# Reordering batch 0's prologue in a fused linear-attention and SwiGLU kernel, with two loads exchanged and one eviction postponed

One core of a Trainium2 chip. The metric is device time in microseconds (us), the median of several executions; lower is better. A "fast run" is one not in a slow state.

## The reference

Linear attention with the feature map phi(x) = elu(x) + 1, then a gated feed-forward block. Batch 8, 8 heads, 576 positions, head size 64; 4608 tokens, model width 512, hidden width 1536; float32 in and out (the kernel multiplies in fp16).

```python
k_p, q_p = phi(k), phi(q)                    # phi(x) = where(x > 0, x, exp(x) - 1) + 1
kv  = einsum('bhsd,bhse->bhde', k_p, v)
z   = sum(k_p, axis=2)
x   = (q_p @ kv) / (q_p @ z + 1e-6)          # heads side by side: 4608 x 512
out = (silu(x @ w_gate) * (x @ w_val)) @ w_out
```

phi(k) is computed as max(k, 0) + min(exp(k), 1): `kp` holds the max, `ek` the min, and `add_k` puts their sum into `kp`. A matmul that sums over positions can therefore take the sum, or the two terms one after the other into the same accumulator.

## The kernel before

Everything runs in a hand-written order: each engine executes its instructions in the order of the program. Batch 0 is done first, as fast as possible, to give the first layer ("layer 1", `l1`) its input; from then on TensorE is busy without a break. Heads are handled in two halves (`lp` 0 and 1). PSUM is the memory that TensorE writes its results to; copying a result out of it frees the tile, and is called an eviction. The helpers that matter:

```python
def warm(n, w=512, ps=None): ...             # matmuls on ones: keep TensorE's clock up, result unused
def add_k(b, lp): ...                        # VectorE: kp += ek
def mn_k(b, lp): ...                         # VectorE: ek = min(ek, 1)
def zt(b, lp, ps, t, first, last): ...       # TensorE: column sums of t (9 matmuls of 2 columns)
def zr_copy(b, lp, ps): ...                  # VectorE: scaled copy of the sums, Zr
def kv_corner(b, lp, t, first, last): ...    # TensorE: k.v of a half, 36 matmuls of 64x64
def r_copy(b, l0, l1, engs): ...             # k.v out of PSUM, R
def t_corners(g, W, lp, ps): ...             # TensorE: q times Zr (denominator) or R (numerator)
def lnrd(ps, i): ...                         # ScalarE: 1/denominator as exp(-log)
def x_t(g, lp, ps): ...                      # VectorE: numerator times that: x, two chunks
def l1_mm(g, fb, ps, chunks): ...            # TensorE: layer 1, gate and value, on some of x's 4 chunks
```

The loads' order and the stretch of batch 0 that the change touches:

```python
    ...
    ld_w1(1280, 1536)
    ld(k, kr, 1, 1)
    ld_w2(0, 4)
    ld(q, qr, 1, 0)
    ld_w2(4, 8)
    ld(q, qr, 1, 1)
    ld_w2(8, 12)
    ld2(v, vr, 1)
    ...
    zt(0, 0, X[1], kp, True, False)
    warm(WARM[3])
    zt(0, 0, X[1], ek, False, True)
    zr_copy(0, 0, X[1])
    warm(WARM[4])
    t_corners(0, Zr, 0, pp4[2])
    lnrd(pp4[2], 0)
    q_phi(1, 1, qb)
    mn_k(0, 1)
    zt(0, 1, Y[0], kp, True, False)
    warm(WARM[5])
    zt(0, 1, Y[0], ek, False, True)
    add_k(0, 0)
    zr_copy(0, 1, Y[0])
    warm(WARM[6])
    kv_corner(0, 0, kp, True, True)
    t_corners(0, Zr, 1, Y)
    lnrd(Y, 1)
    r_copy(0, 0, 1, "VV")
    add_k(0, 1)
    t_corners(0, R, 0, X)
    x_t(0, 0, X)
    kv_corner(0, 1, kp, True, True)
    r_copy(0, 1, 2, "VV")
    warm(WARM[7], ps=pp4[2][1])
    l1_mm(0, 0, pp4[2], (0,))
    l1_mm(0, 1, X, (0,))
    t_corners(0, R, 1, pp4[1])
    x_t(0, 1, pp4[1])
    for c in (1, 2, 3):
        l1_mm(0, 0, pp4[2], (c,))
    ...
```

The end of layer 2 of period 0, where the input of period 1 is made (`nx`) between output tiles:

```python
        for t in range(4):
            ...
            if t == 3:
                nx(0, dz)                    # corners and the x products of period 1
                nx(1, cq)
            for fb in range(FO, FB):
                l2_mm(0, t, fb)
            if t < 3:
                l2_out(0, t, "V")            # VectorE: output tile out of PSUM
        exp_k(2, 0)
        exp_k(2, 1)
        l2_out(0, 3, "V")
```

## Time and profile before

| | before |
|---|---|
| median of three runs | 314.52 us (314.24 to 314.89) |
| span of the traced run | 312.5 us |
| first scale copy `Zr` (VectorE) | 10.11 us |
| first layer-1 matmul | 14.34 us |
| layer 1 in steady state (17th layer-1 matmul) | 18.28 us |
| layer 2 starts, first transposes | 35.54, 40.77 us |
| first and third layer-1 matmul of period 1 | 49.84, 50.44 us |

All times in the traces count from the start of the span. The first loads land at slightly different times in each execution, and shift all that follows (the first scale copy starts at 9.96 to 10.55 us in the traces below). So I compare stretches between two events of one trace: from the first scale copy to steady layer 1 (8.16 us before), the idle time ahead of the first transposes (their start, less the start of the matmul before them, less 0.216), and from the transposes to the third matmul of period 1 (9.67). The profile's lines are in the prediction.

### The profile page before, as it was taken

What the parts mean: (1) busy time and instruction counts of PE and PEld (TensorE: products, weight loads), DVE (VectorE), ACT (ScalarE), POOL (GpSimd) and SP (SyncE); (2) the same over time, 40 slices, a digit from 0 to 9 for tenths busy, and PEclk for the clock granted to TensorE, in tenths of its full rate; (3) what the DMA queues carried; (4) which work ended last, traced back from release to release, by engine and by line L of the source; (5) the groups of instructions that cost most, each with busy time, mean ns of one, the idle gap of its engine ahead of it and who ended that gap; (6) DMA issues with size and microseconds to landing.
All of it is one profiled execution on the core that took longest, in us unless ns stands there. A gap on an engine that the chain in (4) does not pass through costs nothing.

```text
span 312.5 us, 5494 instructions
## 1 busy us (share of the span) xinstructions
PE 306.2 (98%) x2169; PEld 142.3 (46%) x2169; DVE 204.0 (65%) x361; ACT 153.9 (49%) x232; POOL 47.4 (15%) x72
## 2 busy tenths in 40 slices
PE   8999999999999999999999999999999999999994
PEld 3444454444544454445444544454444444444442
DVE  4854859899699657976697759874981434143410
ACT  4955869639733845375535643475330333133311
POOL 8655334310000410032000500000000000000000
PEclk9999999999999999999999999999999999999999
DMA  8999999997512594139612990324032300140014
GB/s 218 198 196 200 207 206 240 231 206 127 116 26 41 92 192 117 38 50 183 171 37 39 131 235 3 73 45 92 2 69 57 86 1 1 39 97 0 0 36 101
DMA packets 41162, 32.80 MB, mean 105 GB/s; under 512 B 16432, under 2 KB 36144, under 8 KB 41136
## 3 DMA queue, kind: packets, MB, share of 16 engines
q0 software_dynamic: 20464, 18.29, 37.4%
q1 hardware_dynamic: 20592, 14.13, 18.8%
q8 instruction: 17, 0.28, 0.4%
q14 instruction: 9, 0.07, 0.1%
q10 hardware_dynamic: 80, 0.03, 0.0%
HBM read 37.75 MB, written 9.44 MB: 151 GB/s over the span
## 4 chain that ended last, share of the span: by engine, by line
PE 95%; DMA 1%; DVE 1%; ACT 1%; issue 0%; SPq 0%; DVEq 0%
PE pp L292 57%; PE pp L299 30%; PE pp L276 2%; PE pp L254 2%; PE pp L185 2%; DMA q<-in_q_dram 1%; PE pp L124 0%; ACT ek L120 0%; PE pp L398 0%; PE pp L370 0%; PE pp L429 0%; DVE xT L411 0%; ACT qT L120 0%; DVE kp L159 0%; PE pp L212 0%
## 5 line engine op out<-in xcount | busy, mean ns | idle before, releaser
L120 ACT ACTIVATE sil<-pp 128x512 f16<-128x512 f32 x108 | 63.4, 597 | 101.8 <-PE pp L292 100.0
L292 PE MATMUL pp<-xT,wg 128*128 128x512 f16 x416 | 106.8, 379 | 0.0
L292 PE MATMUL pp<-xT,wv 128*128 128x512 f16 x416 | 106.8, 379 | 0.0
L285 DVE SCALAR_TENSOR_TENSOR hT<-pp,sil 128x512 f16<-128x512 f32 x108 | 72.4, 681 | 48.8 <-PE pp L292 35.5
L299 PE MATMUL pp<-wo,hT 128*128 128x512 f16 (+2 forms) x444 | 97.1, 373 | 0.6 <-DVE osb L322 0.6
L299 PEld LDWEIGHTS <-hT 128*128 128x128 f16 x444 | 42.0, 98 | 49.8 <-issue 2.1
L292 PEld LDWEIGHTS <-wv 128*128 128x128 f16 x416 | 40.7, 98 | 49.1
L292 PEld LDWEIGHTS <-wg 128*128 128x128 f16 x416 | 40.7, 98 | 48.4
L322 DVE TENSOR_SCALAR osb<-pp 128x512 f32<-128x512 f32 (+1 forms) x19 | 12.9, 682 | 30.9 <-PE pp L299 26.5
L120 ACT ACTIVATE osb<-pp 128x512 f32<-128x512 f32 (+1 forms) x18 | 10.3, 574 | 34.8 <-PE pp L299 34.8
L120 ACT ACTIVATE ek<-kr 128x1152 f16<-128x1152 f16 x16 | 17.9, 1157 | 0.1
L120 ACT ACT_TABLE_LOAD x13 | 16.7, 1283 | 2.3 <-PE pp L292 2.1
L229 DVE TENSOR_TENSOR qp<-qp,rden 128x1152 f16<-128x1152 f16 x12 | 16.2, 1347 | 0.0
L220 DVE TENSOR_REDUCE den<-prod 128x18 f32<-128x1152 f16 x12 | 16.1, 1343 | 0.0
L120 ACT ACTIVATE eq<-qr 128x1152 f16<-128x1152 f16 (+1 forms) x15 | 16.0, 1102 | 0.1
L695 POOL COPY gate<-qT 128x1 f16<-128x1 f16 x4 | 1.0, 256 | 97.2 <-DMA qT<-qp 97.2
L271 DVE TENSOR_SCALAR xT<-pp 128x512 f16<-128x512 f32 (+1 forms) x14 | 8.8, 667 | 7.1 <-PE pp L254 7.1
L103 POOL DMA_DIRECT2D vr<-in_v_dram x16 | 11.7, 731 | 8.5 <-PE pp L292 2.6
L103 POOL DMA_DIRECT2D kr<-in_k_dram x16 | 11.5, 723 | 8.9 <-DMA vr<-in_v_dram 2.8
L159 DVE TENSOR_TENSOR kp<-ek,kp 128x1152 f16<-128x1152 f16 x16 | 12.1, 758 | 0.5
L103 POOL DMA_DIRECT2D qr<-in_q_dram x14 | 10.3, 736 | 6.7 <-DMA wo<-in_moe_w_out_dram 1.7
L147 DVE TENSOR_SCALAR ek<-ek 128x1152 f16<-128x1152 f16 x16 | 7.5, 470 | 5.7 <-ACT ek L120 5.5
(82 smaller groups left out, 179.5 us busy)
## 6 DMA issues: line engine op xcount, KB each, us to landing
out_dram<-osb SPq DMA_DIRECT2D x70, 128.0 KB, 3.4
kr<-in_k_dram POOLq DMA_DIRECT2D x16, 288.0 KB, 8.6
vr<-in_v_dram POOLq DMA_DIRECT2D x16, 288.0 KB, 9.9
qr<-in_q_dram POOLq DMA_DIRECT2D x14, 288.0 KB, 11.9
wo<-in_moe_w_out_dram POOLq DMA_DIRECT2D x3, 512.0 KB, 13.0
wg<-in_moe_w_gate_dram POOLq DMA_DIRECT2D x5, 256.0 KB, 8.7
wv<-in_moe_w_val_dram POOLq DMA_DIRECT2D x5, 256.0 KB, 9.3
q<-in_q_dram SPq DMA_DIRECT2D x2, 576.0 KB, 4.1
```

The costliest lines, as they stand in the source:

```text
L103: nc.gpsimd.dma_start(out=dst[b % NB][:, 2 * lp:2 * lp + 2, :], in_=src[b].rearrange("(l a) (c j) d -> (a c) l (j d)", a=2, j=J)[:, 2 * lp ...
L120: nc.scalar.activation(out=out, in_=in_, func=func, bias=bias, scale=scale)
L147: nc.vector.tensor_scalar(out=a, in0=a, scalar1=1.0, scalar2=None, op0=ALU.min)
L159: nc.vector.tensor_tensor(out=a, in0=ek[b % 2][:, lp, :, :], in1=a, op=ALU.add)
L185: nc.tensor.matmul(out=ps[hh][D * l2:D * l2 + D, D * lp:D * lp + D], lhsT=t[b % 2][rows, lp, j, D * l2:D * l2 + D], rhs=vr[b % NB][rows, 2 ...
L220: nc.vector.tensor_reduce(out=den[:, c, :], in_=prod[:, :, :].rearrange("p j (l d) -> p (j l) d", d=D), axis=AX.X, op=ALU.add)
L229: nc.vector.tensor_tensor(out=qv, in0=qv, in1=rden[:, c, :].unsqueeze(2).to_broadcast([P, 2 * J, D]), op=ALU.mult)
L271: nc.vector.tensor_scalar(out=dst, in0=ps[l2][:, c0:], scalar1=1.0 / SC, scalar2=None, op0=ALU.mult)
L285: nc.vector.scalar_tensor_tensor(out=hT[g % 2][:, fb, :], in0=ps[1][:, :], scalar=SC, in1=s[:, :], op0=ALU.mult, op1=ALU.mult)
L292: nc.tensor.matmul(out=ps[h][:, :], lhsT=w[:, c, P * fb:P * fb + P], rhs=xT[g % 2][:, c, :], start=(c == 0), stop=(c == 3))
L299: nc.tensor.matmul(out=l2p[(g, t)][:, n0:n1], lhsT=hT[g % 2][:, fb, P * t:P * t + P], rhs=wo[:, fb, n0:n1], start=(fb == 0), stop=(fb == F ...
L322: nc.vector.tensor_scalar(out=o[:, n0:n1], in0=ps[:, n0:n1], scalar1=1.0 / SC, scalar2=None, op0=ALU.mult)
```

## The change

Its intent: take the second half's addition off VectorE by giving TensorE the two terms, bring the first k.v and the first x forward, let w_out's second third arrive before q's first half, and let period 1's x go ahead of an output eviction.

```diff
--- before.py
+++ after.py
@@ -40,7 +40,7 @@
     EPS = 1e-6
     SC = 4096.0
     NB = 3
-    WARM = (4, 1, 4, 3, 2, 1, 1, 1)
+    WARM = (4, 1, 4, 4, 2, 2)
 
     sb = ctx.enter_context(tc.tile_pool(name="sb", bufs=1))
     pp = ctx.enter_context(tc.tile_pool(name="ps", bufs=1, space=bass.MemoryType.PSUM))
@@ -345,8 +345,8 @@
     ld_w1(1280, 1536)
     ld(k, kr, 1, 1)
     ld_w2(0, 4)
+    ld_w2(4, 8)
     ld(q, qr, 1, 0)
-    ld_w2(4, 8)
     ld(q, qr, 1, 1)
     ld_w2(8, 12)
     ld2(v, vr, 1)
@@ -474,24 +474,22 @@
     warm(WARM[4])
     t_corners(0, Zr, 0, pp4[2])
     lnrd(pp4[2], 0)
+    add_k(0, 0)
     q_phi(1, 1, qb)
-    mn_k(0, 1)
     zt(0, 1, Y[0], kp, True, False)
     warm(WARM[5])
+    kv_corner(0, 0, kp, True, True)
+    r_copy(0, 0, 1, "VV")
+    mn_k(0, 1)
+    t_corners(0, R, 0, X)
     zt(0, 1, Y[0], ek, False, True)
-    add_k(0, 0)
     zr_copy(0, 1, Y[0])
-    warm(WARM[6])
-    kv_corner(0, 0, kp, True, True)
     t_corners(0, Zr, 1, Y)
     lnrd(Y, 1)
-    r_copy(0, 0, 1, "VV")
-    add_k(0, 1)
-    t_corners(0, R, 0, X)
     x_t(0, 0, X)
-    kv_corner(0, 1, kp, True, True)
+    kv_corner(0, 1, kp, True, False)
+    kv_corner(0, 1, ek, False, True)
     r_copy(0, 1, 2, "VV")
-    warm(WARM[7], ps=pp4[2][1])
     l1_mm(0, 0, pp4[2], (0,))
     l1_mm(0, 1, X, (0,))
     t_corners(0, R, 1, pp4[1])
@@ -639,10 +637,11 @@
                 nx(1, cq)
             for fb in range(FO, FB):
                 l2_mm(0, t, fb)
-            if t < 3:
+            if t < 2:
                 l2_out(0, t, "V")
         exp_k(2, 0)
         exp_k(2, 1)
+        l2_out(0, 2, "V")
         l2_out(0, 3, "V")
         exp_q(2, 0)
         exp_q(2, 1)
```

## The prediction

> **What bounds the kernel now.** I read the page first, then the chain of waits from 0 to 45 us, then the timeline of TensorE, VectorE and ScalarE instruction by instruction from 9.6 to 19 us and from 40 to 52 us, then the landing records of the loads.
>
> ```profile
> PE 306.2 (98%) x2169; PEld 142.3 (46%) x2169; DVE 204.0 (65%) x361; ACT 153.9 (49%) x232; POOL 47.4 (15%) x72
> ...
> PE 95%; DMA 1%; DVE 1%; ACT 1%; issue 0%; SPq 0%; DVEq 0%
> ```
>
> The first line is busy time by engine, the second the chain that ended last. Of it 95% is TensorE, at full clock in every slice. Each full 512-column matmul starts 0.2155 us after the one before. So after the prologue a change only matters where it opens or closes a hole between two TensorE instructions, and a microsecond is 0.3% of the time. The holes that the diff touches are before 18.28 us (where the steady first layer starts) and near 50 us.
>
> Chain of waits (start, us, what), the stretch that the diff reorders:
>
> ```profile
> 11.43 0.38 PE pp L398 x9
> 11.81 0.24 PE pp L124
> 12.05 0.04 issue
> 12.09 0.55 PE pp L185 x36
> 12.63 0.34 DVE R L201 x2
> 12.98 0.68 DVE kp L159
> 13.66 0.04 issue
> 13.70 0.48 PE pp L185 x36
> 14.18 0.32 PE pp L124
> 14.50 0.86 PE pp L276 x4
> ```
>
> L185 is k.v for one half, L201 its copies, L159 the addition that completes k for a half, L124 a warming matmul, L276 the first layer-1 matmuls. The VectorE timeline of the same stretch (start, us):
>
> ```profile
> 11.28 0.75 DVE L159 TENSOR_TENSOR kp<-ek,kp 128x1152 f16<-128x1152 f16 x1
> 11.95 0.28 DVE L402 TENSOR_SCALAR Zr<-pp 128x128 f16<-128x128 f32 x1
> 12.62 0.36 DVE L201 CAST R<-pp 128x64 f16<-128x64 f32 x2 [0.39 <-PE pp L185]
> 12.90 0.75 DVE L159 TENSOR_TENSOR kp<-ek,kp 128x1152 f16<-128x1152 f16 x1
> 13.56 1.28 DVE L411 SCALAR_TENSOR_TENSOR xT<-pp,rd 128x512 f16<-128x512 f32 x2
> ```
>
> The first x chunk (L411) ends at 14.25 and layer 1 starts at 14.34: x is what it waits for. Later, around the hand-over to period 1 (timeline, VectorE and TensorE):
>
> ```profile
> 48.50 0.69 DVE L322 TENSOR_SCALAR osb<-pp 128x512 f32<-128x512 f32 x1 [0.18 <-PE pp L299]
> ...
> 49.84 0.38 PE L276 MATMUL pp<-xT,wg 128*128 128x512 f16 x1
> 50.06 0.38 PE L276 MATMUL pp<-xT,wv 128*128 128x512 f16 x1
> 50.44 0.38 PE L276 MATMUL pp<-xT,wg 128*128 128x512 f16 x1
> ```
>
> The output eviction L322 runs to 49.20 ahead of the four x products, the first of which starts at 49.11. The last layer-2 matmul starts at 49.41, so TensorE is free at 49.62 but starts at 49.84; its next chunk waits again (50.06 to 50.44 instead of 0.216).
>
> **What the Trainium skill says.** "VectorE: DVE Perf Modes", section "Side-by-side: where the cycles go for N=2048 bf16": about 150 cycles plus elements over 1, 2 or 4 per cycle at 0.96 GHz, a two-tensor operation reaching 2. Estimate for 1152 fp16: 0.76 us; the trace has 0.75 for L159, and 0.45 for the one-source min and max. So the dropped addition is worth 0.75, of which 0.67 shows on VectorE because successive instructions overlap by about 0.08. "TensorEngine Tiling (Array Packing)", section "Key Properties": changing the tiling mode drains the array. The trace agrees: four concurrent 64x64 matmuls at 10.47 are followed by a 128x128 one at 10.80, 0.33 where 0.216 would do, so a switch is about 0.12. "TensorE: Matmul & The Clock Gate", part 1: the clock halves after an idle window of about 3.4 us. The warming matmuls are 17 before and 17 after and no new hole exceeds 0.6 us by my count, so I expect no change of clock; the trace of before shows full clock throughout. "DMA: Bandwidth & Descriptors", section "Issuing engines are not separate DMA queues": all loads share 16 engines. The trace has them above 90% busy to about 45 us at 204 GB/s, so an exchange of two loads moves bytes, it does not make them faster.
>
> **The prologue, step by step (by the measured spacings of before).** Up to the scale copy L402 at 10.11 to 10.41 nothing moves: the extra warming matmul there fits ahead of the wait for the min (8.74 + 4 x 0.2155 = 9.60, the wait ends at 9.69). Then, in the new order:
> - VectorE: add of the first half 10.32 to 11.07 (before 11.28 to 12.04). The q product follows, to 11.68.
> - TensorE: column sums of k's max at 10.80, warming matmuls at 11.06 and 11.27 (two now, one before), free at 11.49, mode switch, k.v at 11.58. It could have started at about 11.15 without the two; still 0.51 earlier than 12.09. Copies 12.12 to 12.47 (0.535 after k.v's start, as before).
> - Min of the second half 12.39 to 12.84. Corners with R 12.40 to 12.93.
> - Column sums of the min: 12.84 + 0.055 = 12.89, results at 13.28 (nine matmuls, 0.39). Before they started at 11.43. They now stand behind k.v, its copies and the min.
> - Scale copy L402 13.32 to 13.61 (before 11.95). Denominator corners 13.67. x products: VectorE takes the first at 13.53, only 0.03 earlier than the 13.56 of before, although its corners are there at 12.93: the column sums' round trip has taken the place of the addition.
> - k.v of the second half, now 72 matmuls at 0.0079 each: about 13.90 to 14.49 as starts (same mode, 0.22 after the denominator corners). Before: 13.70 to 13.99.
> - Layer 1 after a mode switch: 14.62, its x having been ready at 14.21. Before 14.34. The four matmuls, the corners, and the other twelve follow at the spacings of before; the copies (14.75 to 15.10) are in time.
> - The logarithm chain on ScalarE starts at about 14.1 instead of 13.40 and ends at 16.7 instead of 15.97. The x product that needs it last starts at about 16.8 and ends at 17.5, the chunk that reads it is wanted at 17.7: just in time.
>
> So the addition saved (0.67) and the earlier k.v (0.51) do not reach layer 1; the doubled k.v (36 x 0.0079 = 0.28) and the later column sums do. The start of steady layer 1 moves from 18.28 to about 18.57: **+0.3 us**, uncertain by 0.15.
>
> **w_out ahead of q.** The landing records give w_out's first third 34.07, q first half 35.49, w_out's second third 37.98, q second half 39.42. Exchanged: w_out at 36.63 (34.07 + 2.56), q at about 38.0. The second third is wanted when the fifth of the layer-2 blocks starts, 35.54 + 16 x 0.2165 = 39.0: it had 1.0 us to spare, so nothing is won. The first half of q is wanted by the max at 37.84 and the exponential at 38.16; with TensorE, and these with it, 0.3 later, the max is wanted at 38.14 and q is just there. Were the prologue faster instead, q would hold the max, and the transposes that follow it (wanted at 40.73, released at 40.77, no slack) with it. Cost 0, up to 0.2.
>
> **The postponed eviction.** Without it the first x product can start when its corners are done (48.81) and the waits are processed, about 48.93 instead of 49.11: 0.18 us. Layer 1 follows at 49.66 and its second chunk at 50.26 instead of 50.44. Gain **-0.18**. The evictions then run 51.3 to 52.6; the tiles they free are wanted again at 54.3 by the fourth block, so no new wait. After that TensorE is again the only bound and passes shifts on one to one.
>
> Sum: +0.3 + 0.05 - 0.18 = +0.17; 314.52 + 0.17 = 314.7, which I move down 0.1, to 314.6, because the kernel before had been tuned and the order was presumably chosen for a gain.
>
> **Rivals.** (a) The prologue gains: if the column sums returned before the corners, x would start at about 13.0 and layer 1 be held only by the second k.v. For it: the addition is on the chain. Against: VectorE and TensorE keep program order, and the scale copy stands ahead of x. Time then 314.1 to 314.3, less whatever q's later landing takes back. (b) q becomes the bound: landing 0.3 later than I reckon, or the prologue 0.3 faster, stalls the transposes by as much; alone 314.8. (c) ScalarE becomes the bound: its chain is 0.7 later; if x's last chunk slipped by 0.3 more, 314.9. (d) Nothing adds up because the differences are as large as the scatter of before (314.24 to 314.89): 314.5.
>
> **Range and chances.** All of these lie between 314.1 and 315.1. Two per cent is 6.3 us, twenty times the largest term, so faster or slower by that takes an event that I don't see, such as a clock drop.
>
> **What would show it.** Right: k.v near 11.6, scale copy near 13.3, first x near 13.5, first layer-1 matmul near 14.6, steady layer 1 near 18.6, a ScalarE gap of 0.6 near 13.5, first x of period 1 about 0.18 sooner after its corners. Wrong: first layer-1 matmul at 14.3 or sooner; TensorE idle ahead of the first transposes near 41 because of q; a slower clock; a wait for w_out.

## The result

| | before | after |
|---|---|---|
| median (4 runs each, alternating) | 314.58 us (314.24 to 314.89) | 314.99 us (314.69 to 315.38) |
| ratio of the fast runs | | 1.0014, 95% interval 0.9997 to 1.0031 |
| ratio in a second series (5 and 9 runs) | | 1.0011, 0.9999 to 1.0024 |
| span of the traced run | 312.5 | 313.6 |

A ratio is the mean time of one kernel's fast runs over that of the other's of the same rounds, so not quite the ratio of the medians that I quote. By either series the change costs 0.35 to 0.45 us (0.0011 and 0.0014 of 314.5), and each interval just includes no difference. The traced execution is the slowest of the changed kernel's four (315.38); its span is 1.1 us over the trace of before.

The page of the changed kernel, busy time and the chain that ended last:

```profile
PE 306.5 (98%) x2205; PEld 142.7 (46%) x2205; DVE 203.4 (65%) x360; ACT 154.1 (49%) x232; POOL 47.6 (15%) x72
...
PE 85%; DMA 10%; POOL 1%; DVE 1%; issue 0%; ACT 0%; POOLq 0%
```

There are 36 more matmuls and one VectorE instruction fewer, as intended. TensorE's share of the chain fell from 95% to 85%, because a load is now on it. VectorE in the prologue (start, us, engine, line, operation):

```profile
10.64 0.75 DVE L159 TENSOR_TENSOR kp<-ek,kp 128x1152 f16<-128x1152 f16 x1
...
12.43 0.36 DVE L201 CAST R<-pp 128x64 f16<-128x64 f32 x2 [0.44 <-PE pp L185]
12.70 0.45 DVE L147 TENSOR_SCALAR ek<-ek 128x1152 f16<-128x1152 f16 x1
13.64 0.29 DVE L402 TENSOR_SCALAR Zr<-pp 128x128 f16<-128x128 f32 x1 [0.48 <-PE pp L398]
13.85 1.28 DVE L411 SCALAR_TENSOR_TENSOR xT<-pp,rd 128x512 f16<-128x512 f32 x2
```

TensorE of the same kernel, same columns:

```profile
11.90 0.48 PE L185 MATMUL pp<-vr,kp 64*64 64x64 f16 x36
12.71 0.54 PE L254 MATMUL pp<-qT,R 64*64 64x512 f16 x4 [0.34 <-DVE R L201]
13.21 0.39 PE L398 MATMUL pp<-ob,ek 128*128 128x2 f16 x9
13.98 0.41 PE L254 MATMUL pp<-qT,Zr 64*64 64x512 f16 x4 [0.38 <-DVE Zr L402]
14.22 0.51 PE L185 MATMUL pp<-vr,kp 64*64 64x64 f16 x36
14.55 0.48 PE L185 MATMUL pp<-vr,ek 64*64 64x64 f16 x36
14.96 0.39 PE L276 MATMUL pp<-xT,wg 128*128 128x512 f16 x1
...
17.41 0.38 PE L276 MATMUL pp<-xT,wv 128*128 128x512 f16 x1
17.73 0.38 PE L276 MATMUL pp<-xT,wg 128*128 128x512 f16 x1
...
42.00 0.62 PE L370 MATMUL pp<-id,qp 128*128 128x128 f16 x8 [0.36 <-DVE qp L377]
```

The first scale copy is at 10.43 here, 0.32 later than in the trace of before, because k landed later; take that off. Then k.v stands at 11.58, the second scale copy at 13.32, the first x at 13.53 and layer 1 at 14.64: the prediction's 11.58, 13.32, 13.53 and 14.62. Two things in this list its sum did not have (the second it had named as a rival and as a sign of being wrong): 17.41 to 17.73 is 0.32 where 0.216 is the rule, with no wait named, and the transposes at 42.00 come after 0.53 us without work. The second is explained on VectorE and in the chain of waits:

```profile
39.15 0.46 DVE L374 TENSOR_SCALAR qp<-qr 128x1152 f16<-128x1152 f16 x1 [0.48 <-DMA qr<-in_q_dram]
...
50.14 2.48 DVE L411 SCALAR_TENSOR_TENSOR xT<-pp,rd 128x512 f16<-128x512 f32 x4 [0.59 <-PE pp L254]
```

```profile
26.11 13.01 DMA qr<-in_q_dram
39.13 0.02 issue
39.15 0.46 DVE qp L374
```

q's first half landed at 39.13, not at 38.0. The second line of the first fence is the postponed eviction at work: the x products follow the corners, with nothing between.

### The profile page after: what moved, and what is told of

The parts are those of the page before. It is cut to its first block, busy times and chain, and to the rows that moved or that the text cites. A ratio compares the mean times of both kernels' runs of the same rounds, so it can differ in the third digit from the quotient of the medians.

```text
span 313.6 us, 5563 instructions
## 1 busy us (share of the span) xinstructions
PE 306.5 (98%) x2205; PEld 142.7 (46%) x2205; DVE 203.4 (65%) x360; ACT 154.1 (49%) x232; POOL 47.6 (15%) x72
## 4 chain that ended last, share of the span: by engine, by line
PE 85%; DMA 10%; POOL 1%; DVE 1%; issue 0%; ACT 0%; POOLq 0%
PE pp L292 52%; PE pp L299 29%; DMA qr<-in_q_dram 4%; DMA kr<-in_k_dram 3%; DMA vr<-in_v_dram 3%; PE pp L254 2%; PE pp L185 2%; PE pp L276 1%; POOL kr L103 0%; POOL wv L112 0%; PE pp L370 0%; DVE qp L377 0%; DVE kp L159 0%; POOL wg L112 0%; POOL vr L103 0%
## 5 line engine op out<-in xcount | busy, mean ns | idle before, releaser
L159 DVE TENSOR_TENSOR kp<-ek,kp 128x1152 f16<-128x1152 f16 x15 | 11.4, 758 | 0.5
```

What stands on the lines that cost most here:

```text
L159: nc.vector.tensor_tensor(out=a, in0=ek[b % 2][:, lp, :, :], in1=a, op=ALU.add)
```

## The experiments

Twelve kernels in three calls (each on another chip), all correct. The results in one table; each kernel's ratio is to the kernel before, on the same chip and in the same rounds. "Prologue" is first scale copy to steady layer 1; "hole" is what the spacing ahead of TensorE's matmul number 224 exceeds 0.216 by, where that matmul falls among the first sixteen of layer 1; "idle" is that ahead of the first transposes; "period 1" is transposes to third matmul of period 1. All from the traces, one execution each. From the third matmul of period 1 to the end the fourteen traces take 262.07 to 262.38 us: the hand-overs near 80 and 145 us lose up to 0.15 us each in some of them, as much as some of the effects (more under e1).

| kernel | prologue | hole | idle | period 1 | ratio, 95% interval |
|---|---|---|---|---|---|
| before | 8.16 | - | 0.04 | 9.67 | |
| the change | 8.59 | 0.10 | 0.53 | 9.49 | 1.0014 (0.9997 to 1.0031) |
| the change again, r1 | 8.87 | 0.38 | 0.20 | 9.48 | 1.0011 (0.9999 to 1.0024) |
| e1 eviction only | 8.17 | - | 0.04 | 9.48 | 0.9994 (0.9981 to 1.0006) |
| e2 w_out only | 8.16 | - | 0.04 | 9.67 | 1.0007 (0.9994 to 1.0019) |
| e3 prologue only | 8.74 | 0.25 | 0.24 | 9.67 | 1.0015 (1.0003 to 1.0028) |
| e4 all but w_out | 8.49 | 0 | 0.04 | 9.48 | 1.0012 (0.9998 to 1.0026) |
| p1 e4 without two warming matmuls | 8.32 | 0.31 | 0.04 | 9.48 | 0.9988 (0.9975 to 1.0001) |
| p2 e4 with the addition back | 8.56 | - | 0.04 | 9.49 | 1.0006 (0.9991 to 1.0020) |
| n2 new order, two terms | 8.11 | 0.67 | 0.04 | 9.48 | 0.9992 (0.9979 to 1.0004) |
| n4 new order, addition | 7.64 | - | 0.25 | 9.49 | 0.9975 (0.9961 to 0.9988) |
| n5 n4 with w_out ahead of q | 7.64 | - | 1.10 | 9.48 | 1.0009 (0.9996 to 1.0021) |
| n6 n4 with q ahead of k | 7.64 | - | 0.00 | 9.47 | 0.9979 (0.9966 to 0.9992) |
| f1 before, 38 more short matmuls | 10.10 | 0.05 | 0.04 | 9.67 | 1.0008 (0.9987 to 1.0029) |

### First call: the parts alone

**e1**, the eviction alone:

```diff
-            if t < 3:
+            if t < 2:
                 l2_out(0, t, "V")
         exp_k(2, 0)
         exp_k(2, 1)
+        l2_out(0, 2, "V")
         l2_out(0, 3, "V")
```

> The kernel before with the postponed output eviction alone. My theory: the first x product of period 1 starts about 0.18 us after its corners are done sooner than before, the gap between the second and third matmul of the first chunk pair stays but everything behind it is 0.18 us earlier; time 0.2 us below before (ratio 0.9994), prologue and transposes unchanged. Rival (the evictions are free where they stood, or come back as a later wait for the tiles they free): no change or a new TensorE wait near 54 us.

Median 314.30 against 314.61 of before. The trace has the x products and then the two evictions on VectorE:

```profile
49.08 2.48 DVE L411 SCALAR_TENSOR_TENSOR xT<-pp,rd 128x512 f16<-128x512 f32 x4 [0.59 <-PE pp L254]
51.48 1.28 DVE L322 TENSOR_SCALAR osb<-pp 128x512 f32<-128x512 f32 x2
```

Period 1 is reached 0.19 us sooner (9.48 against 9.67), in this and in every kernel with this edit, and no wait for the freed tiles appears near 54 us. But at the next hand-over, near 80 us, TensorE loses 0.09 to 0.13 us against the trace of before, in gaps too short for the profile to name a wait: in nine of the ten traces with this edit (not in n6), in none of e2, e3 and f1, which are without it. So about half of the gain stays; the cause is not known. The gain at period 1 is shown by the traces; the time (-0.2 by the ratio) has an interval that includes both zero and half the gain.

**e2**, the loads alone:

```diff
+    ld_w2(4, 8)
     ld(q, qr, 1, 0)
-    ld_w2(4, 8)
```

> The kernel before with w_out's second third ahead of q alone. My theory: the first half of q lands at about 38.0 us instead of 35.5, the max that needs it starts 0.2 us late or more, and TensorE idles 0.2 to 0.6 us ahead of the first transposes (wanted at 40.73); time +0.2 to +0.5 us. Rival (q is in time, or a late landing in the profiled run of the change was an accident of that run): no idle time there, time unchanged.

My expectation of idle time failed: q landed at 38.13 and its max started at 38.15, where the same instruction would have been free to start at 38.06 (the 37.84 of before, plus the 0.22 by which all this trace lies later). The transposes came 0.04 late, as before. Median 314.82 against 314.61; the interval of the ratio (0.9994 to 1.0019) takes in no difference.

**e3**, the prologue alone, and **e4**, the change with the loads of before. Both as edits of the changed kernel; e4 has the first hunk only, e3 both:

```diff
+    ld(q, qr, 1, 0)
     ld_w2(4, 8)
-    ld(q, qr, 1, 0)
     ...
-            if t < 2:
+            if t < 3:
                 l2_out(0, t, "V")
     ...
-        l2_out(0, 2, "V")
```

> The kernel before with the new order of batch 0 alone (loads and eviction as before). My theory: steady layer 1 starts 0.3 to 0.45 us later after the first scale copy than before (before: 8.17 us after it), and nothing later changes; time +0.3 to +0.45 us. Rival (the prologue gains and the loss is all q's landing): 0.2 to 0.5 us faster than before.

> The changed kernel with the loads put back in the order of before. My theory: +0.1 to +0.25 us over before, that is 0.2 to 0.4 us faster than the changed kernel, with no TensorE idle time ahead of the first transposes. Rival (the load order does not matter, or w_out now comes late): as slow as the changed kernel, or a wait for w_out at the fifth block of layer 2.

e3: median 314.96, ratio 1.0015 with an interval above 1: the new order alone costs about 0.47 us (0.0015 of 314.6), as much as the change as far as the intervals tell. The rival falls. Its prologue is 0.58 longer, more than the 0.3 to 0.45 that I expected, and 0.25 of it is a hole. e4: median 314.95 (1.0012, or 0.38 us), over the 0.1 to 0.25 that I expected, though its interval takes that in, and not distinguishable from the change. Its prologue is 0.33 longer than before, without the hole that the others have. So one trace gives the bare chain (+0.33), and the other three with this order, less their holes, give the same 8.49; the rest comes and goes.

### Second call: the chain, the hole, and a better order

**r1**, the changed kernel again.

> The changed kernel again, to stand on the same chip as the next ones and to give a second trace. My theory: prologue +0.3 to +0.45 us (steady layer 1 8.5 to 8.75 us after the first scale copy), eviction -0.19, and an idle stretch ahead of the first transposes that is as long as q's first half lands after about 38.3 us in that run (0.53 us in the first trace, where it landed at 39.13; 0 where it lands by 38.2); time +0.2 to +0.5 us over before.

Median 314.81. q landed at 38.40, in time for its max at 38.87; so the 0.20 us of idle are not q's landing here. VectorE's min of q took 0.61 us where it took 0.45 in the traces of before and of the change. But the prologue lost 0.38 us at a place that no semaphore explains (TensorE's timeline):

```profile
17.41 0.38 PE L276 MATMUL pp<-xT,wv 128*128 128x512 f16 x1
18.01 0.38 PE L276 MATMUL pp<-xT,wg 128*128 128x512 f16 x1 [0.22 <-issue]
```

The page's idle is shorter (0.22) because matmul ends are modelled; the starts are 0.60 apart instead of 0.216. The hole is behind the tenth layer-1 matmul, as in the changed kernel's first trace and in e3.

**p1**, e4 without the two warming matmuls ahead of the first k.v:

```diff
-    WARM = (4, 1, 4, 4, 2, 2)
+    WARM = (4, 1, 4, 4, 2, 0)
```

> The changed kernel with the loads of before and without the two warming matmuls ahead of the first k.v. My theory (layer 1 hangs on one chain: k.v, copies, min, column sums, scale copy, then the corners and the second k.v): k.v starts 0.4 us sooner after the first scale copy (1.07 instead of 1.47), all the rest follows, steady layer 1 starts 8.05 to 8.15 us after it instead of 8.49, time 0.25 to 0.35 us below before. Rival (the logarithm chain on ScalarE or a load bounds the prologue): k.v moves but steady layer 1 stays at 8.4 to 8.5. Second rival: without them the clock falls, and matmuls of 512 columns start 0.43 us apart instead of 0.216.

k.v starts 0.99 us after the scale copy instead of 1.47, and all behind it follows: first layer-1 matmul 4.06 after it, 4.54 in e4. The prologue is 8.32, of which 0.31 is the hole, so 8.01 for the chain alone. Median 313.96 against 314.51, ratio 0.9988 (0.38 us below before); the chain without the hole, with the eviction's 0.19 and 0.1 lost again near 80 us, gives 8.01 - 8.16 - 0.19 + 0.1 = about -0.25. Steady layer 1 itself missed the 8.05 to 8.15 that I expected, by the hole. The chain theory holds, and the full clock was kept (the mean granted clock was 0.997). Here the hole is behind the twelfth layer-1 matmul: two matmuls fewer in the program ahead of layer 1, two later among layer 1. **It is always ahead of TensorE's matmul number 224.**

**n2**, a new order on the kernel before, with e1's eviction: nothing waits behind k.v's copies that does not need them.

```diff
     t_corners(0, Zr, 0, pp4[2])
     lnrd(pp4[2], 0)
-    q_phi(1, 1, qb)
+    add_k(0, 0)
     mn_k(0, 1)
+    q_phi(1, 1, qb)
     zt(0, 1, Y[0], kp, True, False)
-    warm(WARM[5])
+    kv_corner(0, 0, kp, True, True)
     zt(0, 1, Y[0], ek, False, True)
-    add_k(0, 0)
-    zr_copy(0, 1, Y[0])
-    warm(WARM[6])
-    kv_corner(0, 0, kp, True, True)
-    t_corners(0, Zr, 1, Y)
-    lnrd(Y, 1)
     r_copy(0, 0, 1, "VV")
-    add_k(0, 1)
+    zr_copy(0, 1, Y[0])
     t_corners(0, R, 0, X)
     x_t(0, 0, X)
-    kv_corner(0, 1, kp, True, True)
+    t_corners(0, Zr, 1, Y)
+    lnrd(Y, 1)
+    kv_corner(0, 1, kp, True, False)
+    kv_corner(0, 1, ek, False, True)
     r_copy(0, 1, 2, "VV")
-    warm(WARM[7], ps=pp4[2][1])
```

(and WARM = (4, 1, 4, 4, 2))

> A new order for batch 0 on the kernel before, with the postponed eviction and the loads of before: addition of the first half and the min of the second ahead of the q product, k.v at once, column sums right behind k.v and not behind its copies, x behind the scale copy and ahead of the second denominators, last k.v from two terms. My estimate from the spacings of before: k.v 1.03 us after the first scale copy, first x at 2.75 after it, first layer-1 matmul at 3.5 (4.22 before), then the logarithm chain holds the last x, steady layer 1 7.5 to 7.7 us after the scale copy (8.16 before). Time 0.7 to 0.9 us below before. Rival (w_out's second third or a late instruction takes it back): a TensorE wait at the fifth layer-2 block, and 0.3 to 0.5 below.

k.v at 1.01, first x at 2.75 and layer 1 at 3.49 us after the scale copy, as worked out. But the prologue is 8.11, because the hole is 0.67:

```profile
16.32 0.38 PE L276 MATMUL pp<-xT,wv 128*128 128x512 f16 x1
17.21 0.38 PE L276 MATMUL pp<-xT,wg 128*128 128x512 f16 x1 [0.51 <-issue]
```

The rival had named a late instruction beside w_out, but looked for the wait in layer 2 (no trace waits for w_out there). Median 314.27 against 314.51: 0.25 us below before by the ratio, short of my 0.7 to 0.9 and a little short of the rival's 0.3 to 0.5.

**n4**, n2 with the addition and one k.v of 36 matmuls:

```diff
     zr_copy(0, 1, Y[0])
+    add_k(0, 1)
     t_corners(0, R, 0, X)
     ...
-    kv_corner(0, 1, kp, True, False)
-    kv_corner(0, 1, ek, False, True)
+    kv_corner(0, 1, kp, True, True)
```

> As the new order with the eviction, but with the second half completed by the addition again and one k.v of 36 matmuls. My theory: the addition costs 0.2 us at the first layer-1 matmul but the end is set by the logarithm chain, so steady layer 1 is at most 0.1 us later than with two terms; and with 72 fewer TensorE instructions the hole of 0.10 and 0.25 us that two of the three traces with two terms show at the tenth layer-1 matmul is gone. Time within 0.1 us of the two-term version. Rival (the dropped addition is what the change was worth): 0.4 to 0.7 us slower than with two terms.

VectorE of n4:

```profile
12.07 0.28 DVE L402 TENSOR_SCALAR Zr<-pp 128x128 f16<-128x128 f32 x1
12.27 0.74 DVE L159 TENSOR_TENSOR kp<-ek,kp 128x1152 f16<-128x1152 f16 x1
12.93 1.28 DVE L411 SCALAR_TENSOR_TENSOR xT<-pp,rd 128x512 f16<-128x512 f32 x2
```

The addition fits where x would mostly have waited: x starts at 2.97 instead of 2.75 us after the scale copy. The prologue is 7.64, without a hole. **Median 313.75 against 314.51 of before and 314.81 of the change in the same call; ratio 0.9975, interval below 1. This version beats both.** My expectation of a tie with n2 failed: in this order the addition is cheaper than its replacement, by 0.53 us, and no run of the two overlaps (313.58 to 313.85 against 314.18 to 314.30).

### Third call

**p2**, the changed kernel (e4) with the addition put back behind the min:

```diff
     mn_k(0, 1)
+    add_k(0, 1)
     t_corners(0, R, 0, X)
     ...
-    kv_corner(0, 1, kp, True, False)
-    kv_corner(0, 1, ek, False, True)
+    kv_corner(0, 1, kp, True, True)
```

> The changed kernel with the loads of before and with the addition of the second half put back, in VectorE's idle time behind the min, so that the last k.v is one of 36 matmuls. If the two terms cost what I now think (0.28 us of matmuls, and 72 more TensorE instructions that bring TensorE's matmul number 224, where six of the seven traces with two terms have a hole of 0.10 to 0.67 us, into layer 1 before its instructions have arrived): steady layer 1 starts 8.25 to 8.4 us after the first scale copy, no hole among the sixteen first layer-1 matmuls, and the median is 0.1 to 0.4 us below the version with two terms (which stood 0.0012 over before). Rival (the two terms pay for themselves, since the addition takes 0.67 us of VectorE): 0.2 us or more slower than with two terms.

(The expectation miscounts: at that time six traces had two terms, and five of them a hole.) No hole, as expected. But the prologue is 8.56, not 8.25 to 8.4: the second scale copy now comes 3.55 us after the first, where e4 has 3.21. Of these 0.34 us the addition's part is 0.22. The other 0.12 belong to the min ahead of it, which took 0.57 us here and 0.45 in e4; it began shortly after GpSimd had begun to issue a load (GpSimd, then VectorE):

```profile
11.99 0.74 POOL L112 DMA_DIRECT2D wv<-in_moe_w_val_dram  x1 [0.79 <-DMA vr<-in_v_dram]
12.42 0.57 DVE L147 TENSOR_SCALAR ek<-ek 128x1152 f16<-128x1152 f16 x1
```

Without that the prologue would be about 8.44 (an estimate), near e4's 8.49. Median 314.75, ratio 1.0006: between before and e4, and not distinguishable from either. So in the change's own order a gain from putting the addition back is not shown.

**f1**, the kernel before with more instructions and no change of dependency:

```diff
-    warm(WARM[2])
+    warm(42, w=2)
```

> The kernel before, with the four warming matmuls of 512 columns that follow the q transposes replaced by 42 of 2 columns: 38 more matmuls and weight loads, no more time, no dependency touched. If the hole is a late delivery of TensorE's instructions at a fixed place in its program: a hole right ahead of matmul number 224, which is now the first of the third chunk of layer 1 (16.6 us), as long as the delivery takes (the instruction packet of 16 KB at 15.0 to 15.6 us plus 2.2 to 2.5): 0.5 to 1.2 us, and the time 0.4 to 1.2 us over before. Rival (the hole comes from the new order of batch 0): no hole, time unchanged.

No hole at matmul 224 (0.046 us, the wait for x that is there before too), and four of its six runs are at 314.24 to 314.62: the expectation fails. It had taken the packet's time as fixed. The trace says why that is wrong: the instruction packet that stands at 14.8 to 15.6 us in the other kernels is at 12.76 here, 6.2 us ahead of matmul 224. More on that below. The traced execution was also its slowest run (316.69), for another reason: by the trace's clock record TensorE ran at half its clock from 10.74 to 17.56 us, matmuls of 512 columns starting 0.43 apart:

```profile
15.86 0.63 PE L276 MATMUL pp<-xT,wg 128*128 128x512 f16 x1
16.28 0.63 PE L276 MATMUL pp<-xT,wv 128*128 128x512 f16 x1
```

So its prologue of 10.10 says nothing on the hole. The other five runs were granted a mean clock of 0.998 to 1.0 and took 314.24 to 314.82.

**n5**, n4 with e2's edit, and **n6**, n4 with batch 1's first q half ahead of its second k half:

> The fastest version so far (new order of batch 0, completed by the addition, postponed eviction; 0.9975 of before) with w_out's second third ahead of q. My theory: here layer 2 starts 0.7 us sooner than before, so q is missed by more than in the changed kernel: its first half lands at about 38.2, the max that needs it is wanted at 37.2, and the transposes wait about 1 us; time 0.6 to 1.1 us over the fastest version. Rival (w_out bounds the faster version, and its earlier landing is worth something): same or faster.

VectorE, then TensorE, of n5:

```profile
38.43 0.46 DVE L374 TENSOR_SCALAR qp<-qr 128x1152 f16<-128x1152 f16 x1 [1.05 <-DMA qr<-in_q_dram]
```

```profile
41.27 0.62 PE L370 MATMUL pp<-id,qp 128*128 128x128 f16 x8 [0.93 <-DVE qp L377]
```

q landed at 38.41, as in r1; the transposes idle 1.10 us, and the median is 314.81: 1.07 us over n4 by the ratios (1.0009 less 0.9975, of 314.5). The exchange of the loads does not merely fail to help; the faster the prologue, the more it costs.

```diff
-            exp_k(1, 1)
             exp_q(1, 0)
+            exp_k(1, 1)
     ...
             mx_p(0)
-            mn_k(1, 1)
-            add_k(1, 1)
             mn_q(1, 0)
             add_p(0)
+            mn_k(1, 1)
+            add_k(1, 1)
```

> The fastest version so far with batch 1's first q half ahead of its second k half, in both ScalarE's exponentials and VectorE's products. My estimate: the product that releases the first transposes ends 0.5 to 1.1 us sooner, so the idle stretch ahead of them (0.25 us in the trace of the fastest version, 0.04 in that of before) goes, and with it any late VectorE operation; time 0.05 to 0.25 us below the fastest version. Rival: k's half is now late for the column sums and k.v near 43 us, and the idle time moves there.

The idle time is gone in the trace (0.25 to 0.00), and none appears near 43 us, but the median is 314.02 (313.44 to 314.21), ratio 0.9979: not distinguishable from n4. The gain of the edit is not shown.

## Why the prediction was right, and where it was not

The predicted 314.6 lay 0.4 under the measured 314.99 and 0.2 under the second series' 314.81; the range (314.1 to 315.1) held both. That tells little, as the range is 1.0 us wide, more than twice the change: the +0.1 that was forecast is too small against the 0.35 to 0.45 measured. By its steps:

**The prologue's chain: right, in mechanism and size.** Predicted: the column sums' round trip behind k.v replaces the addition, and steady layer 1 is 0.3 us later. The change's events lie within 0.02 us of the predicted ones once k's later landing is taken off, and e4, the trace without a hole, is +0.33. p1 showed that the prologue hangs on that chain (0.48 sooner at its head, 0.48 at the end, less the hole), and n2 and n4 that it was the order that cost, not the idea of an earlier k.v. ScalarE too went as predicted (a gap of 0.62 us, the logarithms from 14.11 to 16.70, with 0.32 taken off). One reading was not right, without harm to the sum: before the change, layer 1 did not wait for x. Its first matmul at 14.34 follows the warming matmul at 14.11 at about the ordinary spacing, as the chain of waits in the prediction has it; x had ended at 14.25, and in n4 layer 1 starts 0.05 us after the end of x.

**A step was missing: a hole behind the doubled k.v, most likely from instructions that arrive late.** I priced the two terms at 0.28 us of matmuls. They also cost a hole: 0.10, 0.38, 0.25, 0.31 and 0.67 us in five of six traces with two terms, 0 in the sixth (e4), always ahead of matmul 224, with no wait for data. The Trainium skill, "Runtime: NRT & Kernel Launch", section "Instruction fetch mechanics", says that an engine refills its instructions in 16 KiB blocks of 256 by DMA while it executes. The traces agree on the packet: they hold one of 16 KB on an instruction queue at 14.97 to 15.60 us in all six, and matmul 224 starts 2.24 to 2.50 us after it in all six, whether that makes a hole or (e4: 2.50, at 17.51) no more than it would start anyway. In the seven traces with one term and the ordinary beginning (before, e1, e2, p2, n4, n5, n6) the packet is at 14.79 to 15.55 and matmul 224 starts 9.4 to 10.2 us after it. (The record does not name the engine that these packets are for; that they are TensorE's is argued from the timing that follows.)

What f1 adds: the packet's time moves with the instructions that came before. Counted from a matmul it stands still: in all fourteen traces, f1's too, it starts 4.28 to 4.74 us after the start of matmul 73 (the one for which I found the least spread). In the five traces with a hole, matmul 224 starts 6.90 to 7.22 us after matmul 73. The change's order needs 6.82 to 6.84 us for this stretch without the hole (e4 has just that), n2's faster order 6.23, which is why n2 has the largest hole; f1 needs 10.7 and the seven others 13.9 to 14.7. What brings matmul 224 so near is the second term: 36 more matmuls within 0.3 us, where the other kernels have layer-1 matmuls 0.216 us apart. That the instructions from matmul 224 on are asked for at a fixed place of the program, and come some 7 us later, fits all fourteen traces. It is argued from them, not isolated: no run moved that place, or spread the short matmuls, with all else equal. What is shown is the cost in that order: n2 against n4, with and without the second term, 0.0017 or 0.53 us, although the chain without the hole would favour n2 (8.11 - 0.67 = 7.44 against 7.64).

**The loads: cost predicted as 0 to 0.2; it ranges from 0 to 0.5.** In e2 nothing (q landed at 38.13), in r1 nothing from q itself (38.40, wanted at 38.87), in the change's first trace 0.5 (39.13). The landing that I reckoned, 38.0, was right for a smooth run; in that trace one of the loads' parts fell behind between 20 and 24 us (the last part of a w_gate load landed 2.9 us after the first, 1.35 in the trace of before). The lag stayed: the first part of q's first half landed at 36.77 in that trace and in r1, the last 2.36 us later in the one and 1.63 in the other. The instruction packets seem to be behind this as well. From one of GpSimd's loads to the next, up to 46 us, the lag of the last part grows by more than 0.2 us in 21 of 316 cases of the fourteen traces, and each of the 21 has its first part landing between 0.8 us ahead of and 1.3 us behind the start of a 16 KB packet (21.51 here), where 46 of the 316 lie; in f1, whose first packet is early, one of them is at 12.84. No run tests it.

That the exchange gains nothing was right: no trace of the kernels without it waits for w_out, not even n4, which starts layer 2 0.7 us sooner. n5 is the clean proof of the term's mechanism, my rival (b).

The remaining idle of 0.20 to 0.25 us ahead of the transposes in r1, e3 and n4 goes with one VectorE operation, the min of q, that took 0.61, 0.66 and 0.66 us instead of 0.45. In all three it started 0.32 to 0.36 us after GpSimd had begun to issue a load. The Trainium skill, "SBUF — State Buffer", section "Who interferes with whom", says that VectorE's two-port modes and GpSimd exclude each other, the first comer keeping the ports. The traces agree: the same operation took 0.45 in the traces of before and of the change, where it began ahead of the issue, and in all fourteen traces the 54 max and min operations of this size (128x1152) that began 0.27 to 0.48 us after the start of such an issue took 0.49 to 0.73 us, while none that began less than 0.27 or more than 0.62 us after one took over 0.46. I did not test it by moving an issue.

**The eviction: right at its place, but not passed on whole.** Predicted -0.18; period 1 is reached 0.18 or 0.19 sooner in nine of the ten traces that have the edit (0.20 in the tenth, n6), with no wait for the freed tiles. That TensorE then passes shifts on one to one failed: 0.09 to 0.13 us are lost again near 80 us in nine of the ten, for a reason that stays open.

**The sum.** +0.3 + 0.05 - 0.18 = +0.17 was predicted, and then moved down to +0.1. That last move was wrong: it came from a guess about intent and not from the profile. With the hole's mean over the change's two traces ((0.10 + 0.38) / 2 = 0.24) and the 0.11 lost again near 80 us the sum is 0.33 + 0.24 + 0 to 0.5 - 0.19 + 0.11 = 0.5 to 1.0, against a measured 0.35 to 0.45. It comes out high because the traced executions of the change are the slowest of their series (315.38 and 315.44 us, against medians of 314.99 and 314.81): the holes of a usual run are probably smaller, which no trace shows. The parts by the ratios are less sharp: e1 -0.19, e2 +0.22, e3 +0.47 us, 0.50 together, each with an interval of about 0.4 to each side.

## What to carry to other kernels

When an instruction leaves a chain, look at what stands in its place in the program order of the same engine: here a freed VectorE waited for a TensorE round trip that the reorder itself had moved behind the copies. Replacing one VectorE instruction by dozens of short matmuls can cost more than their time (here up to 0.67 us); look for a hole without a named wait at a fixed matmul number, and for an instruction packet a little ahead of it. And before a load is pulled ahead of another, compare both landings with both wants: the one that has a microsecond to spare (w_out) should not overtake the one that has none.

## What the Trainium skill lacked or had wrong

- "Runtime: NRT & Kernel Launch", section "Instruction fetch mechanics": calls the cost of crossing a block boundary mostly hidden. Here a hole that fits such a crossing was 0.10 to 0.67 us in five of six traces in which 144 TensorE instructions of short matmuls ran just ahead of the packet; the matmul behind it started 2.24 to 2.50 us after the packet's start, and the packet 4.28 to 4.74 us after matmul 73, with the DMA engines over 90% busy. The page does not give that latency.
- "TensorE: Matmul & The Clock Gate", part 1: its table ties the lower clock to an idle window of about 3.4 us (further on, frequent short idle times bring it down as well). In f1's traced run the clock record has half speed from 10.74 to 17.56 us (316.69 against a median of 314.59), though TensorE's longest idle time from 6.5 us to there was 0.32 us; 42 of its matmuls, from 7.41 us, were 2 columns wide. Whether these brought the clock down is not shown; one of six runs did it.
- No page that I found gives the scatter of loads: in two executions of the changed kernel the last part of q's first half landed at 39.13 and at 38.40, the first part at 36.77 in both; nor that the lag grows where an instruction packet runs (all 21 steps of more than 0.2 us).
